# Decode attention: the first K tile in two halves, a quarter of one half on eight DMA engines, and a shorter list of slots that go straight into the result

## The chip, the cores and the metric

The kernel runs on one core of one Trainium2 chip. The metric is the time of one execution on the device in microseconds (us). The profiles are of one execution each, and their span, from the first instruction to the last, is a little shorter than that time.

## The reference: one query position against 65,536 keys

There are 32 query heads and 8 groups of keys and values; four query heads share a group. For each head the kernel forms scores against 65,536 keys of 128 numbers, takes a softmax over them, and sums the values with these weights. All inputs are bf16.

```python
B, Hq, Hkv, Sq, Sk, D = 1, 32, 8, 1, 65536, 128
...
def reference(q, k, v):
    ...
    k = jnp.repeat(k, rep, axis=1)
    v = jnp.repeat(v, rep, axis=1)
    scale = D ** -0.5
    scores = jnp.einsum("bhqd,bhkd->bhqk", q, k) * scale
    p = _softmax(scores, axis=-1)
    return jnp.einsum("bhqk,bhkd->bhqd", p, v)
```

K and V are 134 MB each and are read once. There is one query position, so there are few operations for each byte that is read.

## The kernel before

K and V of a group come in four tiles each (`j`), 64 tiles in all. A tile has 128 partitions; each holds `T` = 128 consecutive keys of `D` = 128 numbers, one contiguous row of 32 KB, so a tile is 4 MB. All tiles share a pool of five buffers, and SyncE issues the loads in the order of use:

```python
    iopool = ctx.enter_context(tc.tile_pool(name="iopool", bufs=5))
    ...
    def load(view, name, cuts=()):
        t = iopool.tile([P, T * D], bf16, name=name, tag="io")
        edges = [0, *cuts, T]
        for lo, hi in zip(edges, edges[1:]):
            nc.sync.dma_start(out=t[:, lo * D:hi * D], in_=view[:, lo * D:hi * D])
        return t

    q4 = const.tile([P, D], bf16)
    for a in range(NQ):
        nc.scalar.dma_start(out=q4[a * QP:(a + 1) * QP, :], in_=q[0, :, 0, :])

    seq = [("k", 0, j) for j in range(NQ)]
    for g in range(Hkv):
        for s in range(NQ):
            if g + 1 < Hkv:
                seq.append(("k", g + 1, s))
            seq.append(("v", g, s))
```

The query is loaded four times by ScalarE's queue, 32 rows each, transposed, and written into `Z`, from which TensorE takes its weights. A K tile is transposed by VectorE in four parts, and each part is multiplied by TensorE:

```python
    def k_step(g, j):
        kt = load(k_view[g, j], "kt")
        ...
        for i2 in range(0, NI, 2):
            kT = ktp.tile([P, 2 * CW * D], bf16, name="kT")
            nc.vector.transpose(
                out=kT[:, :].bitcast(i32),
                in_=kt[:, i2 * CW * D:(i2 + 2) * CW * D].bitcast(i32),
            )
            # [cut: eight matmuls with weights Z into S]
```

After four K tiles of a group come its softmax (`E`) and, beside the K tiles of the next group, the products of E with its V tiles into the PSUM tiles `A`. `collect` sums the parts of `A` into `ps_f`, four rows of 128 numbers, and `store` scales these and writes them out. The last V tile of all is handled apart. It comes in five pieces, of 64, 32, 16, 8 and 8 of the 128 slots (a slot is one of the `T` keys in each partition):

```python
    CUTS = (T // 2, 3 * T // 4, 7 * T // 8, T - T // 16)   # 64, 96, 112, 120
    EDGE = CUTS[-2]                                         # 112
    ...
    def store(g, ps_f, dma):
        o = stats.tile([HPG, D], bf16, name="o")
        nc.vector.tensor_scalar_mul(out=o[:, :], in0=ps_f[:, :], scalar1=rl_tiles.pop(g)[:, :])
        dma.dma_start(out=out[0, g * HPG:(g + 1) * HPG, 0, :], in_=o[:, :])

    def last_step(g, j):
        vt = load(v_view[g, j], "vt", CUTS)
        ...
        ps_f = collect(g, False)
        for t in range(EDGE):
            s = t % NQ
            slot(t, Dp[s * QP:s * QP + HPG, :], t < NQ, t >= EDGE - NQ)
        Ds = stats.tile([P, D], fp32, name="Ds")
        nc.vector.tensor_copy(out=Ds[:, :], in_=Dp[:, :])
        for t in range(EDGE, CUTS[-1]):
            slot(t, ps_f[:, :], False, False)
        nc.tensor.matmul(
            out=ps_f[:, :], lhsT=selh[:, :], rhs=Ds[:, :], start=False, stop=False
        )
        for t in range(CUTS[-1], T):
            slot(t, ps_f[:, :], False, t == T - 1)
        o = stats.tile([HPG, D], bf16, name="o")
        nc.scalar.mul(o[:, :], ps_f[:, :], rl_tiles.pop(g)[:, :])
        nc.scalar.dma_start(out=out[0, g * HPG:(g + 1) * HPG, 0, :], in_=o[:, :])
```

`slot` is one matmul of 128 columns. The first 112 slots are summed in the PSUM tile `Dp`, in four separate strips of partitions; VectorE copies `Dp` into `Ds`, and one product with `selh` adds its strips into `ps_f`. The last 16 slots go into `ps_f` without this detour.

Of the kernel before, what the change touches and what calls it, by code (L numbers as in the profile page):

```python
# [13 lines left out]
bf16 = mybir.dt.bfloat16  # L14
# [4 lines left out]
def kernel(  # L19
# [19 lines left out]
    nc = tc.nc  # L39
    P = nc.NUM_PARTITIONS  # L40
    B, Hq, Sq, D = q.shape
    _, Hkv, Sk, _ = k.shape
    HPG = Hq // Hkv
    assert B == 1 and Sq == 1 and D == P and HPG == 4 and Hq == 32
    NQ = 4
    QP = 32
    T = Sk // (NQ * NQ * QP)
# [7 lines left out]
    iopool = ctx.enter_context(tc.tile_pool(name="iopool", bufs=5))  # L55
# [4 lines left out]
    stats = ctx.enter_context(tc.tile_pool(name="stats", bufs=2))  # L60
# [4 lines left out]
    k_view = k[0].rearrange("g (j p t) d -> g j p (t d)", j=NQ, p=P)  # L65
    v_view = v[0].rearrange("g (j p t) d -> g j p (t d)", j=NQ, p=P)
# [5 lines that stand above are left out]
            nc.sync.dma_start(out=t[:, lo * D:hi * D], in_=view[:, lo * D:hi * D])  # L72
        return t

    q4 = const.tile([P, D], bf16)
    for a in range(NQ):
        nc.scalar.dma_start(out=q4[a * QP:(a + 1) * QP, :], in_=q[0, :, 0, :])
# [2 lines left out]
    for g in range(Hkv):  # L80
# [9 lines left out]
        out=sel[:, :], in_=ident[:, :].rearrange("p (s c) -> p c s", s=NQ),  # L90
        axis=AX.X, op=ALU.add,
    )
    selh = const.tile([P, HPG], fp32)
    nc.vector.tensor_reduce(
        out=selh[:, :], in_=sel[:, :].rearrange("p (i h) -> p h i", h=HPG),
# [11 lines left out]
    for a in range(NQ):  # L107
        r = slice(a * QP, (a + 1) * QP)
        z0 = QP - HPG + a * QP
        for b in range(2):  # L110
            for e in range(2):
                nc.vector.tensor_copy(  # L112
                    out=Z[r, b, e, :, z0:z0 + HPG], in_=qT_v[r, b, e, :, :]
# [4 lines left out]
    rl_tiles = {}  # L118
    A_tiles = {}

    def k_step(g, j):
        kt = load(k_view[g, j], "kt")
        if j == 0:
            S_tiles[g] = pss.tile([P, NQ, 512], fp32, name="S")
        S = S_tiles[g]
# [6 lines that stand above are left out]
            kT_v = kT[:, :].rearrange("q (i c b p e) -> q i b e c p", i=2, b=2, p=QP, e=2)  # L132
            for i in (i2, i2 + 1):
                w0 = QP - HPG - i * HPG
                for be in range(4):
                    b, e = be // 2, be % 2
                    nc.tensor.matmul(  # L137
                        out=S[:, j, :NCOL],
                        lhsT=Z[:, b, e, g, w0:w0 + P],
                        rhs=kT_v[:, i - i2, b, e, :, :],  # L140
                        start=(i == 0 and be == 0),
                        stop=(i == NI - 1 and be == 3),
                    )
# [38 lines left out]

    last_a = NQ - 2
    CUTS = (T // 2, 3 * T // 4, 7 * T // 8, T - T // 16)
    EDGE = CUTS[-2]

    def v_step(g, j):
        vt = load(v_view[g, j], "vt")
# [20 lines left out]
    def collect(g, stop):  # L209

        A = A_tiles.pop(g)
        As = [apool.tile([P, HI, D], fp32, name=f"As{u}") for u in range(2)]
        nc.scalar.copy(out=As[0][:, :, :].rearrange("p i d -> p (i d)"), in_=A[0][:, :])  # L213
        nc.vector.tensor_copy(out=As[1][:, :, :].rearrange("p i d -> p (i d)"), in_=A[1][:, :])  # L214
        ps_f = psm.tile([HPG, D], fp32, name="ps_f", tag="misc")
        for i in range(NI):
            nc.tensor.matmul(  # L217
                out=ps_f[:, :], lhsT=sel[:, i * HPG:(i + 1) * HPG],
                rhs=As[i // HI][:, i % HI, :],
                start=(i == 0), stop=(stop and i == NI - 1),  # L220
            )
        return ps_f
# [10 lines that stand above are left out]
        E = E_tiles.pop(g)  # L233
        Dp = psm.tile([P, D], fp32, name="Dp", tag="misc")
        nc.vector.memset(Dp[:, :], 0.0)

        def slot(t, dst, start, stop):
            i, c = t // CW, t % CW
            nc.tensor.matmul(
                out=dst, lhsT=E[:, j, c, i * HPG:(i + 1) * HPG],  # L240
                rhs=vt[:, t * D:(t + 1) * D], start=start, stop=stop,
# [5 lines that stand above are left out]
            slot(t, Dp[s * QP:s * QP + HPG, :], t < NQ, t >= EDGE - NQ)  # L247
        Ds = stats.tile([P, D], fp32, name="Ds")
        nc.vector.tensor_copy(out=Ds[:, :], in_=Dp[:, :])
        for t in range(EDGE, CUTS[-1]):  # L250
            slot(t, ps_f[:, :], False, False)
        nc.tensor.matmul(
            out=ps_f[:, :], lhsT=selh[:, :], rhs=Ds[:, :], start=False, stop=False
        )
        for t in range(CUTS[-1], T):
            slot(t, ps_f[:, :], False, t == T - 1)
        o = stats.tile([HPG, D], bf16, name="o")
        nc.scalar.mul(o[:, :], ps_f[:, :], rl_tiles.pop(g)[:, :])
        nc.scalar.dma_start(out=out[0, g * HPG:(g + 1) * HPG, 0, :], in_=o[:, :])

    for kind, g, s in seq:
        if kind == "k":
            k_step(g, s)
            if s == NQ - 1:
                softmax(g)
        else:
            if g == Hkv - 1 and s == NQ - 1:
                last_step(g, s)
            else:
                v_step(g, s)  # L270
                if s == NQ - 1:
                    store(g, collect(g, True), nc.scalar)
# [30 lines left out]
```

## Time and profile before

| | |
|---|---|
| time, median of 3 | 635.35 us (634.92 to 635.39) |
| span of the profiled execution | 633.6 us |
| read from HBM | 268.47 MB, 424 GB/s over the span |
| TensorE busy | 393.8 us (62%) |
| VectorE busy | 341.0 us (54%) |
| ScalarE busy | 22.8 us (4%) |
| mean granted TensorE clock | 0.814 |

In the profile PE stands for TensorE, DVE for VectorE, ACT for ScalarE and SP for SyncE, and a name with a q behind it is the sequencer of that engine. L and a number is a line of the kernel: L128 transposes K, L239 is the matmul of a slot, L252 the product with `Ds`, L258 the last scaling. The page divides the span into 40 equal slices and gives the busy share of each engine in tenths, and for the DMA engines also the rate. The chain that ended last is followed back from the last instruction, at each step to what released it. A wait is printed as: engine and line, what it waited for, us in total, times, longest.

### The profile page before, as it was taken

The numbers are of one execution on the slowest core, as the hardware profiler recorded it, in microseconds if no ns is written. First come the engines' busy times: TensorE is split into PE (matmuls) and PEld (weight loads), VectorE is DVE, ScalarE is ACT, GpSimd is POOL, SyncE is SP. The second block draws the span as 40 slices with busy tenths as digits, with TensorE's granted clock in tenths as the row PEclk, the third lists the DMA queues.
The fourth block names the chain that finished last, engine by engine and source line by source line (L and its number), as shares of the span: only waits on it lengthen the run. The fifth ranks groups of instructions, "written<-read, shape, count | busy, mean of one in ns | idle before, by whom it ended". The sixth has DMA issues, their size and how long they took to land.

```text
span 633.6 us, 5209 instructions
## 1 busy us (share of the span) xinstructions
PE 393.8 (62%) x2314; PEld 158.1 (25%) x2314; DVE 341.0 (54%) x213; ACT 22.8 (4%) x26; POOL 4.9 (1%) x7
## 2 busy tenths in 40 slices
PE   0586666767467665477753776547775577755745
PEld 0232222223122321123221232212321133211323
DVE  0898753766437753467533675345754366553600
ACT  0000100010000100010000100001000010000100
POOL 3000000000000000000000000000000000000000
PEclk9999798758788777986778977789677886877867
DMA  9999999999999999999999999999999999999995
GB/s 370 441 432 430 439 427 432 429 432 427 436 429 430 430 429 430 429 430 430 431 429 429 434 432 430 433 432 432 431 430 429 430 429 430 429 436 430 434 420 220
DMA packets 10071, 268.82 MB, mean 424 GB/s; under 512 B 1344, under 2 KB 1344, under 8 KB 1728
## 3 DMA queue, kind: packets, MB, share of 16 engines
q1 hardware_dynamic: 9792, 268.44, 98.7%
q8 instruction: 18, 0.29, 0.2%
q10 hardware_dynamic: 256, 0.04, 0.0%
q14 instruction: 5, 0.04, 0.0%
HBM read 268.47 MB, written 0.01 MB: 424 GB/s over the span
## 4 chain that ended last, share of the span: by engine, by line
DMA 52%; PE 23%; DVE 17%; issue 7%; ACT 1%; ACTq 0%; SPq 0%; DVEq 0%
DMA kt<-in_k_dram 43%; PE S L137 17%; DVE kT L128 13%; DMA vt<-in_v_dram 6%; PE ps_f L217 3%; PE A L201 2%; DMA q<-in_q_dram 2%; DVE mx L148 2%; DVE As L214 1%; ACT ET L168 1%; PE ps_b L163 0%; DVE o L226 0%; DVE Z L112 0%; PE ps_t L150 0%; PE ps_l L176 0%
## 5 line engine op out<-in xcount | busy, mean ns | idle before, releaser
L137 PE MATMUL S<-kT,Z 128*128 128x512 bf16 x1024 | 294.6, 445 | 187.9 <-DVE kT L128 187.6
L128 DVE STREAM_TRANSPOSE kT<-kt 128x2048 int32<-128x2048 int32 x128 | 289.3, 2292 | 197.6 <-DMA kt<-in_k_dram 155.1
L137 PEld LDWEIGHTS <-Z 128*128 128x128 bf16 x1024 | 111.0, 109 | 370.2 <-issue 295.3
L201 PE MATMUL A<-vt,E 128*32 128x512 bf16 x992 | 67.4, 402 | 10.9 <-DMA vt<-in_v_dram 10.9
L201 PEld LDWEIGHTS <-E 128*32 128x32 bf16 x992 | 26.6, 100 | 47.6 <-issue 27.7
L173 DVE STREAM_TRANSPOSE E<-ET 128x2048 bf16<-128x2048 bf16 x8 | 18.5, 2311 | 17.4 <-ACT ET L168 17.4
L148 DVE TENSOR_REDUCE mx<-S 128x1 f32<-128x2048 f32 x8 | 18.3, 2292 | 15.9 <-PE S L137 15.9
L217 PE MATMUL ps_f<-As,sel 128*4 128x128 f32 x128 | 26.3, 393 | 0.3 <-ACT As L213 0.3
L213 ACT COPY As<-A 128x512 f32<-128x512 f32 x8 | 4.7, 586 | 520.0 <-PE A L201 520.0
L168 ACT ACTIVATE ET<-S,nm 128x2048 bf16<-128x2048 f32 x8 | 15.7, 1968 | 78.4 <-DVE nm L165 78.4
L217 PEld LDWEIGHTS ps_f<-As,sel 128*4 128x4 f32 x128 | 14.6, 118 | 9.4 <-ACT As L213 1.2
L214 DVE COPY As<-A 128x512 f32<-128x512 f32 x8 | 5.5, 692 | 20.6 <-PE A L201 20.2
L176 PE MATMUL ps_l<-ls,selh 128*4 128x1 f32 x16 | 1.5, 165 | 19.1 <-ACT ET L168 19.1
L163 PE MATMUL ps_b<-one,mrow 1*128 1x1 f32 x16 | 3.2, 268 | 10.8 <-DVE mrow L157 10.8
L102 DVE STREAM_TRANSPOSE qT<-q 128x64 int32<-128x64 int32 x1 | 0.2, 245 | 15.9 <-DMA q<-in_q_dram 15.9
L226 DVE TENSOR_SCALAR o<-ps_f,rl 4x128 bf16<-4x128 f32 x7 | 2.4, 339 | 8.3 <-PE ps_f L217 8.3
L150 PE MATMUL ps_t<-ident,mx 128*1 128x128 f32 x8 | 2.2, 270 | 6.3 <-DVE mx L148 6.3
L163 PEld LDWEIGHTS ps_b<-one,mrow 1*128 1x128 f32 x16 | 2.5, 198 | 13.0 <-DVE mrow L157 13.0
L176 PEld LDWEIGHTS ps_l<-ls,selh 128*4 128x4 f32 x16 | 0.7, 84 | 19.8 <-ACT ET L168 19.8
L106 POOL MEMSET Z<- 128x4992 bf16 x1 | 4.3, 4263 | 0.0
L152 DVE TENSOR_REDUCE m<-ps_t 1x4 f32<-1x128 f32 x8 | 2.2, 273 | 2.5 <-PE ps_t L150 2.5
L165 DVE COPY nm<-ps_b 128x1 f32<-128x1 f32 x8 | 1.3, 158 | 4.0 <-PE ps_b L163 4.0
(23 smaller groups left out, 17.0 us busy)
## 6 DMA issues: line engine op xcount, KB each, us to landing
kt<-in_k_dram SPq DMA_DIRECT2D x32, 4096.0 KB, 43.0
vt<-in_v_dram SPq DMA_DIRECT2D x31, 4096.0 KB, 38.0
vt<-in_v_dram SPq DMA_DIRECT2D x1, 2048.0 KB
vt<-in_v_dram SPq DMA_DIRECT2D x1, 1024.0 KB
vt<-in_v_dram SPq DMA_DIRECT2D x1, 512.0 KB
vt<-in_v_dram SPq DMA_DIRECT2D x2, 256.0 KB
out_dram<-o ACTq DMA_DIRECT2D x8, 1.0 KB
q<-in_q_dram ACTq DMA_DIRECT2D x4, 8.0 KB, 6.0
```

The source lines that it names most:

```text
L106: nc.gpsimd.memset(Z[:, :, :, :, :], 0.0)
L128: nc.vector.transpose(out=kT[:, :].bitcast(i32), in_=kt[:, i2 * CW * D:(i2 + 2) * CW * D].bitcast(i32),)
L137: nc.tensor.matmul(out=S[:, j, :NCOL], lhsT=Z[:, b, e, g, w0:w0 + P], rhs=kT_v[:, i - i2, b, e, :, :], start=(i == 0 and be == 0), stop=(i ...
L148: nc.vector.reduce_max(out=mx[:, :], in_=S[:, :, :NCOL], axis=AX.XY)
L163: nc.tensor.matmul(out=ps_b[:, :], lhsT=mrow[:, :], rhs=one[:, :], start=True, stop=True)
L168: nc.scalar.activation(out=ET[:, :].rearrange("p (a n) -> p a n", a=NQ), in_=S[:, :, :NCOL], func=ACT.Exp, bias=nm[:, :], scale=SCALE, acc ...
L173: nc.vector.transpose(out=E[:, :, :, :].rearrange("p a c r -> p (a c r)"), in_=ET[:, :])
L201: nc.tensor.matmul(out=A[u][s * QP:(s + 1) * QP, :], lhsT=E[:, j, c, :], rhs=vt_v[:, u, c, :, :], start=(j == 0 and c0 == 0), stop=(j == e ...
L213: nc.scalar.copy(out=As[0][:, :, :].rearrange("p i d -> p (i d)"), in_=A[0][:, :])
L214: nc.vector.tensor_copy(out=As[1][:, :, :].rearrange("p i d -> p (i d)"), in_=A[1][:, :])
L217: nc.tensor.matmul(out=ps_f[:, :], lhsT=sel[:, i * HPG:(i + 1) * HPG], rhs=As[i // HI][:, i % HI, :], start=(i == 0), stop=(stop and i == ...
L226: nc.vector.tensor_scalar_mul(out=o[:, :], in0=ps_f[:, :], scalar1=rl_tiles.pop(g)[:, :])
```

## The change

The first K tile is no longer one load of 128 rows by 32 KB. Its first half (slots 0 to 63) is one load of 128 rows by 16 KB. Of its second half, rows 0 to 95 are one load, and rows 96 to 127 are four loads of eight rows each, every fourth row: 96, 100, ..., 124, then 97, 101, ..., and so on. The loads of eight rows are meant for DMA engines 0 to 7 alone, so that these carry more bytes of this tile than engines 8 to 15, and the 16 engines finish the whole stream closer together.

At the other end, `EDGE` moves from 112 to 120: the fourth piece of the last V tile goes into `Dp` with those before it, and only the last eight slots go straight into `ps_f`. The product with `Ds` is now the last of the sum, and the result is scaled by VectorE and stored by SyncE, through the same `store` as for the other groups (those by ScalarE's queue), where ScalarE did both for the last group. All else stands in the same order on each engine.

```diff
+    def load_first(view, name):
+        t = iopool.tile([P, T * D], bf16, name=name, tag="io")
+        h, p0 = T * D // 2, P - QP
+        nc.sync.dma_start(out=t[:, :h], in_=view[:, :h])
+        nc.sync.dma_start(out=t[:p0, h:], in_=view[:p0, h:])
+        for r in range(4):
+            nc.sync.dma_start(out=t[p0 + r::4, h:], in_=view[p0 + r::4, h:])
+        return t
 ...
     def k_step(g, j):
-        kt = load(k_view[g, j], "kt")
+        kt = (load_first if g == j == 0 else load)(k_view[g, j], "kt")
 ...
-    EDGE = CUTS[-2]
+    EDGE = CUTS[-1]
 ...
         nc.vector.tensor_copy(out=Ds[:, :], in_=Dp[:, :])
-        for t in range(EDGE, CUTS[-1]):
+        for t in range(EDGE, T):
             slot(t, ps_f[:, :], False, False)
         nc.tensor.matmul(
-            out=ps_f[:, :], lhsT=selh[:, :], rhs=Ds[:, :], start=False, stop=False
+            out=ps_f[:, :], lhsT=selh[:, :], rhs=Ds[:, :], start=False, stop=True
         )
-        for t in range(CUTS[-1], T):
-            slot(t, ps_f[:, :], False, t == T - 1)
-        o = stats.tile([HPG, D], bf16, name="o")
-        nc.scalar.mul(o[:, :], ps_f[:, :], rl_tiles.pop(g)[:, :])
-        nc.scalar.dma_start(out=out[0, g * HPG:(g + 1) * HPG, 0, :], in_=o[:, :])
+        store(g, ps_f, nc.sync)
```

The loads that SyncE issues wait for the transfer that used the same semaphore eight transfers earlier: in the changed kernel the third load of eight rows waits for the first transfer of q, the fourth for the second, the second K tile for the third, and the third K tile for the fourth.

## The prediction

> **What bounds the kernel now.** I read the page first: the forty slices, the DMA queues and the chain that ended last.
>
> ```profile
> DVE  0898753766437753467533675345754366553600
> DMA  9999999999999999999999999999999999999995
> GB/s 370 441 432 430 439 427 432 429 432 427 436 429 430 430 429 430 429 430 430 431 429 429 434 432 430 433 432 432 431 430 429 430 429 430 429 436 430 434 420 220
> ...
> q1 hardware_dynamic: 9792, 268.44, 98.7%
> q8 instruction: 18, 0.29, 0.2%
> q10 hardware_dynamic: 256, 0.04, 0.0%
> q14 instruction: 5, 0.04, 0.0%
> ```
>
> The DMA engines are busy in every slice but the last, at 427 to 441 GB/s; VectorE and TensorE are not. So what counts is when the last of 16 engines delivers its last byte, and what follows. Then the chain in order of time, at both ends, says what those are:
>
> ```profile
> 2.12 14.56 DMA q<-in_q_dram
> ...
> 19.55 2.23 DVE kT L128
> ```
>
> ```profile
> 591.74 37.29 DMA vt<-in_v_dram
> 629.03 0.04 issue
> 629.07 0.61 PE ps_f L239 x8
> 629.68 0.22 PE ps_f L252 x2
> 629.90 0.46 PE ps_f L239 x8
> 630.36 0.02 issue
> 630.38 0.36 ACT o L258
> ```
>
> The columns are start, duration and holder. At the head, compute waits 14.56 us for q and starts on K at 19.55. At the tail, the fourth piece of the last V tile lands at 629.03 and 1.7 us of work follows; the store then takes the rest of the 633.6 us span. The third reading is the waits of the queue that issues the loads:
>
> ```profile
> SPq L72 <- DVE kT L128: 365.9, 32, 19.5
> SPq L72 <- PE A L201: 98.0, 27, 4.5
> ```
>
> It waits for buffers (total, times, longest), but loads take about 40 us from issue to landing (the page's list of issues: 43.0 for K, 38.0 for V), four tiles' worth, so these waits leave no hole in the GB/s row.
>
> Fourth, what the sums hide, from the trace's records of packets and of semaphore landings. A 32 KB packet takes 1.22 us (mean of 8064), so a half row of 16 KB takes 0.61 us. Every tile gives each engine the same bytes, yet the engines drift apart: the fifth K tile, at 51 us, lands within 0.5 us on 15 engines. The last piece of V lands like this (us from the span's start, in order of time):
>
> ```
> 624.96 624.98 625.00 625.05 625.11 625.22 625.62
> 627.82 627.90 627.98 627.99 628.08 628.09 628.11 628.32 629.67
> ```
>
> Seven engines are early, nine late by about 3, one of the nine by 4.7. The 16 KB instruction packets (q8) explain it: one every 24 to 44 us, 1.02 to 1.11 us long, their lengths repeating with a period of eight, and after each one another engine lags by some 1.4 us. Eight engines thus take two each; the seventeenth (612.85 us) makes the latest. Which eight? The store of group 6 is four packets, and three of them (607.22, 607.24, 607.37) sit exactly two 1.22 us packets behind completions of early engines; the fourth belongs to a late one. [...]the early ones are, by all appearance, engines 0 to 7 but one, and the late ones 8 to 15 and that one. I call it X; the 8 KB packets of q14 fit its lag.
>
> [...]No view names an engine[...]. [...]q is 12 packets per engine (8 of data, 4 completions), each behind one of 1.22 us, 12 x 1.22 = 14.6 us, against 14.56 measured. [...]32 KB in 1.22 us is 27 GB/s per engine[...].
>
> **The change part by part.**
> (1) The split. Of the second half, 96 rows over 16 engines are 6 half rows each; four loads of 8 give engines 0 to 7 four more. Engines 0 to 7 carry 8 + 6 + 4 = 18 half rows instead of 16, engines 8 to 15 carry 14: +2 x 0.61 = +1.22 us and -1.22 us, if nothing else limits them. That is meant to take back a lag of 3. The late eight would end at 626.6 to 627.1 and the latest at 629.67 - 1.22 = 628.45. The six early ones go to at most 626.84. But X gets the addition too: 627.9 + 1.22 = 629.12 becomes the last landing. Gain 629.67 - 629.12 = 0.55 us. Sixteen-KB packets cost about 10 ns more each (4 KB takes 0.165 us, 2 KB 0.082); eight are 0.1 us, within the error.
> (2) The head. q's 12 packets now follow packets of 0.61 us: about 7.3 us instead of 14.6, so the first transpose starts near 12.5 us instead of 19.55. Off the path: worth nothing while the transfers are unbroken.
> (3) The tail. Before, the final 0.61 + 0.22 + 0.46 us of TensorE start at the fourth piece (629.03) and cover the landing of the fifth (629.67). Now the fourth piece's 8 slots go to Dp, the copy of Dp (0.29) can run beside the last 8 slots, and the product with Ds comes last. After the last landing: 0.04 + 8 slots 0.6 + product 0.25 + 0.02 + VectorE's scaling 0.34 (its row for the other groups) = 1.25 us. From 629.12 this gives 630.37, against 630.74 before: -0.37. The store from SyncE is issued in 0.33 us where ScalarE took 0.26: +0.07. Sum -0.3.
>
> **The rivals.**
> A, engines set the rate: the sum above, 635.35 - 0.3 = 635.05 us. For it: equal bytes and unequal ends, with the lag following the instruction packets.
> B, [...]the split adds collisions. [...]engines 0 to 7 fall back by about 4.9 us (3.7 to 6.1 by engine), while engines 8 to 15 lose 2.44 and gain 1.22. Early ones would end near 630.5, X at 627.9 + 3.7 to 4.9, that is 631.6 to 632.8, and the latest of the others near 629.67 + 1.22 = 630.9. With 632.3 and the same tail of 1.25 plus 0.07: 633.6 against 630.74, so +2.9, 638.2 us.[...]
> C, a hole in the stream: the third 8-row load waits for q's first transfer, the fourth for the second, the second K tile for the third. With rounds of 0.61 us the third lands near 8.3 us; engines 8 to 15 have work until 1.75 + 0.69 + 14 x 0.61 = 11.0 (0.69 is how much longer the first packet took). An issue lands its first packet about 1.0 us later (0.74 to 1.75 in this trace). Margin 1.7 us, so I expect no hole; it would add about 1 us.
> D, the earlier head counts: at most 19.55 - 12.5 = 7 us, 628 us. The full DMA row and the 40 us of loads in flight speak against it.
>
> **Range and chances.** I give B 55 in 100, A 40, the rest to C and D. That is two heaps, at 635.05 and 638.2; the mean, 636.8, is my prediction, a little slower. The range goes from just under A to above B, 634.6 to 639.2. Two per cent are 12.7 us: even B with a hole and D stay within. Chances: faster 0.01, within 0.98, slower 0.01.
>
> **What would show it right or wrong.** The first transpose near 12.5 us and an unchanged end would confirm (2). The last piece's landings decide between A and B: under A the seven move later by 1.2 and the late ones earlier by 1.2; under B both move later, the seven by 4 to 5. Under B, 16 KB packets around 7 to 17 us take up to 1.2 us instead of 0.61, under A none. A gap between packets near 11 us is C. The tail must hold, after the last landing, 8 slots, 2 products and VectorE's scaling in about 1.25 us. I am wrong if packets stretch elsewhere, if X lies in the other half[...], or if the time leaves the range.

## The result and the profile after

The changed kernel takes 640.79 us (median of 6, 640.67 to 641.32) beside 635.29 us for the kernel before in the same runs: a ratio of 1.0089, 95% interval 1.0076 to 1.0102. That is 5.5 us slower. The prediction had the direction and, in its rival B (the split adds collisions, 55 chances in 100), the kind of cause, but neither its 636.8 us nor B's 638.2 us nor the range up to 639.2 us held.

The page of the changed kernel, the forty slices and the DMA queues:

```profile
DVE  1698655565455653566543766337653467544510
DMA  9999999999999999999999999999999999999995
GB/s 264 394 426 425 427 444 437 426 427 425 428 443 432 433 427 426 427 437 433 434 431 426 428 434 431 432 431 435 428 433 432 431 425 439 430 433 431 426 422 228
...
q1 hardware_dynamic: 9976, 268.44, 98.7%
q8 instruction: 18, 0.29, 0.2%
q10 hardware_dynamic: 248, 0.04, 0.0%
q14 instruction: 4, 0.03, 0.0%
```

The bytes are the same, and from the third slice on the rate is what it was (431 GB/s in the mean of the third to the last but one, in both). The loss is in the first two slices: 264 and 394 GB/s instead of 370 and 441. A slice is 16 us long, so they moved (370 - 264 + 441 - 394) x 16 = 2,450 KB less, which is 5.7 us at 430 GB/s. The DMA row does not show it: it reads 9 there as well. The DMA engines count as busy as before and deliver less.

The busy time by stretch narrows it down. The columns are the stretch, its length, the busy time of PE, its weight loads, DVE, ACT and POOL with counts, the granted clock, the DMA share and the rate. First the kernel before, then the changed one:

```profile
8.00:13.00 5.00, 0.00 (x0) 0.00 (x0) 0.00 (x0) 0.00 (x0) 0.00 (x0) 1.00 0.99 422
14.00:18.50 4.50, 0.00 (x0) 0.00 (x0) 1.56 (x14) 0.00 (x0) 0.00 (x0) 1.00 1.00 431
21.00:31.00 10.00, 8.51 (x27) 3.10 (x27) 8.08 (x5) 0.00 (x0) 0.00 (x0) 1.00 0.99 426
```

```profile
8.00:13.00 5.00, 0.00 (x0) 0.00 (x0) 0.00 (x0) 0.00 (x0) 0.00 (x0) 1.00 1.12 257
14.00:18.50 4.50, 0.00 (x0) 0.11 (x1) 1.77 (x14) 0.00 (x0) 0.00 (x0) 1.00 0.84 171
21.00:31.00 10.00, 7.91 (x24) 2.90 (x24) 8.25 (x5) 0.00 (x0) 0.00 (x0) 1.00 0.98 419
```

From 8 to 13 us the 96-row load runs, from 14 to 18.5 us the four loads of 8 rows beside the next tile. (Bytes are booked in the stretch where a packet begins, so short stretches are rough.) The two stretches move 257 and 171 GB/s where they moved 422 and 431, at a DMA share of 1.12 and 0.84, and from 21 us on the rate is nearly that of before. The records of the packets say the same: after the first one on each engine, 16 KB packets took 0.61 us in the first half of the tile, and 112 of the 128 in its second half took 0.9 to 1.4 us; 16 packets of 32 KB that engines 8 to 15 moved for the next tile took 2.4 to 2.6 us instead of 1.22.

The chain of the changed kernel in order of time, head and tail:

```profile
2.13 10.86 DMA q<-in_q_dram
12.98 0.02 issue
13.00 36.05 DMA kt<-in_k_dram
```

```profile
605.89 29.37 DMA vt<-in_v_dram
635.26 0.04 issue
635.30 1.01 PE ps_f L250 x8
636.31 0.44 PE ps_f L263 x2
636.75 0.03 issue
636.78 0.34 DVE o L237
```

The last landing moved from 629.67 to 635.26 us: 5.6 of the 5.7 us by which the span grew (633.6 to 639.3). What comes after it is nearly as long as before, 639.3 - 635.26 = 4.0 us against 633.6 - 629.67 = 3.9.

The waits of the loads' queue have not changed in kind (total us, times, longest), so nothing holds the stream back from that side:

```profile
SPq L72 <- DVE kT L139: 359.4, 32, 20.0
...
SPq L72 <- PE A L212: 98.0, 27, 4.5
```

**Who lost how much.** The semaphore landings of the second K tile, from the trace's records: before, all 16 engines between 22.24 and 22.74 us. In the changed kernel, two groups of eight:

```
27.00 27.00 27.05 27.06 27.14 27.24 27.25 27.36      (mean +4.7 us)
29.38 29.39 29.41 29.43 29.45 29.48 29.51 29.62      (mean +7.0 us)
```

They are 2.3 us apart, close to 4 x 0.61 = 2.44 us: the four half rows that engines 0 to 7 carry more than engines 8 to 15. So the eight later ones are those that carried the loads of 8 rows: in this trace each of these loads has a group of eight landings (15.89 to 16.36 us for the first), where the 96-row load has 16 (14.56 to 15.58). No record gives an engine's number; engines 0 to 7 is the name of those eight here, 8 to 15 of the others. The bytes did move between the engines as meant, on top of a loss common to all 16 of about (4.7 + 7.0) / 2 = 5.8 us. At the end the two delays persist. The last piece of V lands at

```
629.55 629.76 631.96 631.98 632.03 632.12 632.59 632.61
632.65 632.67 632.75 632.77 634.41 634.93 635.05 635.26
```

Set against the list in the prediction, with +4.7 for one group and +7.0 for the other, this fits only if two of the seven early engines belong to 8 to 15 and five to 0 to 7, and if of the nine late ones three belong to 0 to 7 (634.93, 635.05, 635.26) and six to 8 to 15. The packets of this trace say the same by another way: on one engine a packet's record starts 3 or 4 ns before the end of the one ahead of it, so each engine can be followed from the second tile to the last piece. The 16 KB instruction packets fall on six of the eight early-landing engines of the second tile (8 to 15) and on two of the eight later ones (0 to 7); one more of 0 to 7 has three of the 8 KB ones instead and is late as well. That one is X.

### The profile page after: what moved, and what is told of

Its sections match the earlier page's. It is cut to its first block, busy times and chain, and to the rows that moved or that the text cites. A ratio compares the mean times of both kernels' runs of the same rounds, so it can differ in the third digit from the quotient of the medians.

```text
span 639.3 us, 5216 instructions
## 1 busy us (share of the span) xinstructions
PE 394.3 (62%) x2314; PEld 158.2 (25%) x2314; DVE 341.6 (53%) x214; ACT 22.4 (4%) x25; POOL 4.9 (1%) x7
## 4 chain that ended last, share of the span: by engine, by line
DMA 64%; PE 18%; DVE 12%; issue 5%; ACT 0%; ACTq 0%; DVEq 0%
DMA kt<-in_k_dram 50%; PE S L148 13%; DMA vt<-in_v_dram 11%; DVE kT L139 9%; PE A L212 2%; PE ps_f L228 2%; DVE mx L159 2%; DMA q<-in_q_dram 2%; ACT ET L179 0%; DVE As L225 0%; PE ps_b L174 0%; DVE o L237 0%; PE ps_t L161 0%; ACTq L88 0%; PE ps_f L250 0%
## 5 line engine op out<-in xcount | busy, mean ns | idle before, releaser
L184 DVE STREAM_TRANSPOSE E<-ET 128x2048 bf16<-128x2048 bf16 x8 | 18.5, 2311 | 17.4 <-ACT ET L179 17.4
L225 DVE COPY As<-A 128x512 f32<-128x512 f32 x8 | 5.5, 691 | 18.9 <-PE A L212 18.5
L250 PE MATMUL Dp<-vt,E 128*4 128x128 bf16 x120 | 2.7, 218 | 1.6 <-DMA vt<-in_v_dram 1.6
(22 smaller groups left out, 15.6 us busy)
```

The costliest lines, as they stand in the source:

```text
L184: nc.vector.transpose(out=E[:, :, :, :].rearrange("p a c r -> p (a c r)"), in_=ET[:, :])
```

## The experiments

Four theories were to be told apart. P, after the prediction's rival B: loads hold each other up, depending on the partitions that they go to and on their number of rows, and then run at about half speed. T: part of the loss is the new tail. S or R: the loss is in small pieces or in the number of loads, wherever they go. B (in this section only, and not the prediction's B): the unequal bytes of the engines are the loss. All runs are compared with the kernel before on the same chip; ratios are of times, with 95% intervals.

### The two halves of the change, each alone

**Loads alone**: the changed first K tile with the tail of before.

```diff
-        kt = load(k_view[g, j], "kt")
+        kt = (load_first if g == j == 0 else load)(k_view[g, j], "kt")
```

> The changed loading of the first K tile with the tail of the kernel before. Theory P[...]: the whole loss is here, 635.3 + 5.5 = 640.8 us, and 16 KB packets from 8 to 18 us take about 1.15 us. Rival T (a part of the loss is the new tail, whose last slots ran at half the clock): at least 0.6 us less, 640.1.

Measured: 641.1 us, ratio 1.0089 (1.0074 to 1.0104), the same as the whole change. **Tail alone**: `EDGE = CUTS[-1]`, the product with `Ds` last, and `store` from SyncE.

> The loads of the kernel before with the changed tail. Theory P: 635.3 to 635.5 us, as the slower last slots and the quicker store about cancel. Rival T: 635.9 us or more.

Measured: 635.26 us, ratio 0.9998 (0.9990 to 1.0007). The whole loss is in the loads; T falls. The slow last slots of the changed kernel, 1.01 us for eight where this run needed 0.61, come with a granted clock of half. The stretches of the changed kernel from 634 us:

```profile
634.00:635.30 1.30, 0.68 (x24) 0.39 (x24) 0.29 (x1) 0.00 (x0) 0.00 (x0) 0.99 0.13 44
635.30:636.80 1.50, 1.44 (x10) 0.93 (x9) 0.02 (x1) 0.00 (x0) 0.00 (x0) 0.50 0.00 0
```

The clock reads 0.50 in the second. With the tail alone it stayed at 1.00 at that place:

```profile
629.81 0.04 issue
629.86 0.61 PE ps_f L239 x8
630.46 0.23 PE ps_f L252 x2
630.69 0.02 issue
630.72 0.34 DVE o L226
```

So the new tail can run at the full clock. Whether it runs at half the clock more often is open: of the three profiles with the new tail, two had the product with `Ds` at half the clock (0.44 us here and in the last run below, 0.23 above), and none of the twelve with the old tail had (0.22). In the changed kernel the store landed sooner (1.2 us after its issue, 2.0 before, where an 8 KB instruction packet ran for 0.58 us from 631.41), which about paid it back.

### Halves without a split of rows

```diff
-        kt = load(k_view[g, j], "kt")
+        kt = load(k_view[g, j], "kt", (T // 2,) if g == j == 0 else ())
```

> First K tile in two halves of 128 rows each, nothing moved between engines, tail of before. Theory P: [...]no stretched packets, 635.3 us, although the first transpose starts some 7 us earlier. Rival S (the loss comes from 16 KB pieces or from more loads at the start): 1 us or more above before.

Measured: 635.5 us, ratio 1.0002 (0.9993 to 1.0011). Its stretches:

```profile
8.00:13.00 5.00, 0.00 (x0) 0.11 (x1) 2.10 (x18) 0.00 (x0) 0.00 (x0) 1.00 1.11 474
14.00:18.50 4.50, 3.27 (x8) 1.11 (x8) 3.83 (x4) 0.00 (x0) 0.00 (x0) 1.00 0.89 386
```

There are 16 KB packets here too, those of the second half took 0.61 us each, and the rate over both stretches is whole (474 and 386 beside 422 and 431), so S falls for the pieces. VectorE and TensorE are at work from 13 to 18.5 us (first transpose at 12.87 us, 19.55 before), and 6.7 us of earlier start are worth nothing. That is rival D of the prediction, answered.

### The 96 rows without moved bytes

```diff
         nc.sync.dma_start(out=t[:, :h], in_=view[:, :h])
         nc.sync.dma_start(out=t[:p0, h:], in_=view[:p0, h:])
-        for r in range(4):
-            nc.sync.dma_start(out=t[p0 + r::4, h:], in_=view[p0 + r::4, h:])
+        nc.sync.dma_start(out=t[p0:, h:], in_=view[p0:, h:])
```

> Second half of the first K tile as 96 rows and one load of 32 rows, so that each of 16 engines still gets 6 + 2 half rows: no bytes move between engines. Theory P: the 96 rows lose 2.8 us on all engines as in the changed kernel, the 32 rows[...] another 2 x 0.61 = 1.2: 635.3 + 4.0 = 639.3 us. Rival B (the loss comes from the unequal bytes of engines 0 to 7 and 8 to 15): 635.3 us.

Measured: 640.18 us, ratio 1.0074 (1.0059 to 1.0089). With equal bytes on all engines most of the loss stands; B falls as its cause. The stretch of the 96 rows is as slow as in the changed kernel (257 GB/s there):

```profile
8.00:13.00 5.00, 0.00 (x0) 0.00 (x0) 0.00 (x0) 0.00 (x0) 0.00 (x0) 1.00 1.10 247
```

The time is 0.9 us more than P's sum: the 96 rows lost more than the 2.8 us that I had read off the packets.

### The same load, into other partitions and on its own

Extra loads, issued just ahead of the first V tile (j = 0) of group 3, counted from 0, go into a buffer of the pool that nothing reads; they run at about 283 us. They are work that the kernel does not need; only their cost is looked at.

```diff
+    def extra():
+        t = iopool.tile([P, T * D], bf16, name="xt", tag="io")
+        view = k_view[0, 0]
+        for r in range(4):
+            nc.sync.dma_start(out=t[96 + r::4, :], in_=view[96 + r::4, :])
 ...
     def v_step(g, j):
+        if (g, j) == (3, 0):
+            extra()
         vt = load(v_view[g, j], "vt")
```

> Extra work in mid-stream that nothing reads: four loads of 8 whole rows (32 KB each) of K into partitions 96 to 127, every fourth. Engines 0 to 7 get 4 x 1.22 = 4.88 us more. Theory P: [...]engines 0 to 7 lose 9.8 us and engines 8 to 15 4.9; the latest of engines 0 to 7 ends at 628.1 + 9.8 = 637.9 instead of 629.67: 635.3 + 8.2 = 643.5 us. Rival R (such loads cost what they cost wherever they land): 628.1 + 4.88 = 633.0, 638.6 us, and the same as with partitions 0 to 31.

Measured: 645.03 us, ratio 1.0148 (1.0133 to 1.0163). With `t[r:32:4, :]` and the same rows of `view` instead:

> The same four extra loads of 8 rows, into partitions 0 to 31, every fourth[...]. Theory P: no stretched packets, engines 0 to 7 lose 4.88 us, engines 8 to 15 nothing: 635.3 + 3.3 = 638.6 us. Rival R: the same time as with partitions 96 to 127.

Measured: 638.24 us, ratio 1.0041 (1.0026 to 1.0055). The same number of loads, rows and bytes costs 9.4 us in one place of SBUF and 2.6 in the other. Partitions 96 to 127, then 0 to 31, in the stretch of the extra loads:

```profile
285.00:297.00 12.00, 7.95 (x29) 3.57 (x30) 7.81 (x6) 1.35 (x2) 0.00 (x0) 0.50 0.96 205
```

```profile
285.00:297.00 12.00, 7.84 (x28) 3.44 (x29) 7.70 (x6) 1.46 (x2) 0.00 (x0) 0.50 1.00 429
```

205 GB/s against 429, at a DMA share of 0.96 and 1.00. (The clock of 0.50 is TensorE's; it is the same in both.) R falls.

Then one load of 64 rows, first into partitions 0 to 63:

```diff
+        nc.sync.dma_start(out=t[:64, :], in_=view[:64, :])
```

> Extra load in mid-stream of 64 whole rows into partitions 0 to 63 (4 rows on each of 16 engines[...]). Theory P: half speed, 4 x 2.44 = 9.8 us on all engines, 645.1 us. Rival R: 4 x 1.22 = 4.9 us, 640.2 us.

Measured: 647.17 us, ratio 1.0181 (1.0165 to 1.0196). And with `t[32:96, :]` and the same rows of `view`:

> The same extra load of 64 rows, into partitions 32 to 95[...]. Theory P with rows dealt out in blocks[...] 4.9 us on all, 640.2 us. Theory P with rows dealt out in another way: packets stretched, up to 645.1 us. Rival R: 640.2 us.

Measured: 640.27 us, ratio 1.0073 (1.0058 to 1.0088). Partitions 0 to 63, then 32 to 95:

```profile
285.00:297.00 12.00, 7.83 (x28) 3.50 (x29) 7.70 (x6) 1.47 (x2) 0.00 (x0) 0.50 1.00 216
```

```profile
285.00:297.00 12.00, 7.67 (x28) 3.50 (x29) 7.53 (x6) 1.63 (x2) 0.00 (x0) 0.50 1.01 434
```

216 GB/s is half of 434. Between about 280 and 305 us, 99 packets of 32 KB took over 1.35 us in the first and one in the second (an instruction packet's neighbour). The source rows move with the partitions in these pairs, but rows 0 to 31 and rows 32 to 95 were each read at the full rate and rows 0 to 63 at half, so the source is not the cause. And as the second load cost 4.65 us, no more than the 4.9 us of its bytes, taking a buffer of the pool cost nothing.

### The 96 rows in two places, and 48

The one thing that P as I had it could not say is why all 16 engines went at about half speed under the 96-row load. Two estimates of mine, G1 with some engines at full pace and G2 with all of them losing alike, were put to the test with 96 extra rows, in two places:

```diff
+        nc.sync.dma_start(out=t[32:, :], in_=view[32:, :])     # first run
+        nc.sync.dma_start(out=t[:96, :], in_=view[:96, :])     # second run
```

> Extra load in mid-stream of 96 whole rows into partitions 32 to 127, 6 rows on each engine, 7.3 us without collisions. Theory G2[...]: four rows of each engine collide with none[...]: 9.8 us on all engines, 645.1 us, and about 32 packets of 2.4 us. Theory G1[...]: engines 0 to 5 keep 7.3 us, the others lose 9.8 to 13.4, the latest ends near 642: 647 to 649 us, and packets of 2.4 us on engines 6 to 15 only, from the first row on. Rival R[...]: 642.6 us.

Measured: 652.65 us, ratio 1.0267 (1.0253 to 1.0281).

> The same extra load of 96 rows into partitions 0 to 95. Theory G2: [...]6 x 2.44 = 14.6 us on all 16 engines, 650 us or, as the 64-row load lost a fifth more than its sum, 652; no engine keeps its pace. Theory G1: engines 11 to 15 keep 7.3 us, the rest lose 9.8 to 14.6. Rival R: 642.6 us.

Measured: 651.06 us, ratio 1.0244 (1.0230 to 1.0258). G2 (650 to 652 us) had the second run right, but missed the first by 7.5 us. G1 missed the first by 3.7 us and more, and in the second it had engines 11 to 15 keep their pace: from 284 to 301 us no packet of any engine kept its 1.22 us, in either run. All 16 engines are slow wherever the 96 rows lie. A third estimate, G3, has 96 rows at half speed on all engines in both places, 64 rows as they were found, and 48 rows at a quarter:

```diff
+        nc.sync.dma_start(out=t[:48, :], in_=view[:48, :])
```

> Extra load in mid-stream of 48 whole rows into partitions 0 to 47, 3 rows on each engine, 3.7 us without collisions. Theory G3[...]: [...]a quarter of the speed, 3 x 4.88 = 14.6 us on all engines, 650 us, with packets near 4.9 us. Theory G1[...]: [...]3 x 2.44 = 7.3 us, 643 us, packets up to some 2.5 us. Rival R[...]: 639.2 us.

Measured: 650.84 us, ratio 1.0241 (1.0224 to 1.0258), for half of the bytes of the 96-row load. The stretch of the extra load, with 96 rows (0 to 95) and with 48:

```profile
285.00:297.00 12.00, 8.23 (x32) 3.81 (x33) 8.78 (x6) 1.07 (x2) 0.00 (x0) 0.72 1.00 224
```

```profile
285.00:297.00 12.00, 7.60 (x28) 3.43 (x29) 7.46 (x6) 1.70 (x2) 0.00 (x0) 0.50 1.09 131
```

224 GB/s is about half of the 434 that stood under 64 rows at 32 to 95, 131 not much more than a quarter of it (109). With 48 rows, 44 packets took 4.0 to 4.9 us, with rows 0 to 95 none over 2.6. G3's 650 us was stated before this run and it holds; G1 and R do not. The quarter also speaks against a coarser limit, one rate for each half of the partitions: rows 0 to 47 would then run at half, as rows 0 to 63 did. No other row count was tried, and no record names the rows that an engine takes: G3 fits the three that were, and why they differ was not shown. One thing G3 leaves open: its sum for 96 extra rows is 650 us wherever they lie, and rows 32 to 127 took 652.65 us, with 18 packets of 2.6 to 3.8 us.

### The change mirrored, and the candidate

The 96 rows are now 32 to 127, and the loads of 8 are rows 0 to 31, where the extra loads of 8 rows left the full rate (429 GB/s); the same bytes are moved.

```diff
-        h, p0 = T * D // 2, P - QP
+        h, p0 = T * D // 2, QP
...
-        nc.sync.dma_start(out=t[:p0, h:], in_=view[:p0, h:])
-        for r in range(4):
-            nc.sync.dma_start(out=t[p0 + r::4, h:], in_=view[p0 + r::4, h:])
+        nc.sync.dma_start(out=t[p0:, h:], in_=view[p0:, h:])
+        for r in range(4):
+            nc.sync.dma_start(out=t[r:p0:4, h:], in_=view[r:p0:4, h:])
```

> The change mirrored: the 96 rows are 32 to 127, and the four loads of 8 rows are rows 0 to 31[...]; the same bytes move from engines 8 to 15 to engines 0 to 7. Tail of before. Theory P with G2: the 96 rows lose 1.2 us, the loads of 8 nothing, the late ones of engines 0 to 7 end at 628.1 + 1.2 + 1.2 = 630.5 instead of 629.7: 636.1 us, 4.5 us less than the change. Rival B (the moved bytes themselves are the loss): as slow as the change, 640.8 us.

Measured: 638.8 us, ratio 1.0052 (1.0037 to 1.0068). With the same bytes moved, and as many loads of the same sizes, it loses 3.3 us instead of 5.5: B falls again as the whole cause, though the moved bytes are 1.22 us of the sum below, and the number of loads falls with it. P's 636.1 us was written down with G2 and missed by 2.7 us. With G3, worked out after the run, the 96 rows lose 6 x 0.61 = 3.66 us, the loads of 8 none, and the late ones of engines 0 to 7 end at 628.1 + 3.66 + 1.22 = 632.98; its last landing is at 632.99. The second tile landed 2.4 us later than before on eight engines and 4.7 us on the other eight, against 3.66 - 1.22 = 2.44 and 3.66 + 1.22 = 4.88. Its stretches show one slow part where the change has two:

```profile
8.00:13.00 5.00, 0.00 (x0) 0.00 (x0) 0.00 (x0) 0.00 (x0) 0.00 (x0) 1.00 1.10 244
14.00:18.50 4.50, 0.00 (x0) 0.10 (x1) 2.61 (x15) 0.00 (x0) 0.00 (x0) 1.00 1.14 455
```

What can be kept of the change is the halves and the tail, each free of the loss:

> The candidate without the row split: first K tile in two halves of 128 rows, and the changed tail. Theory P: no loss, 635.2 us, the same as before within 0.1%.

Measured: 635.24 us, ratio 0.9995 (0.9987 to 1.0003). No difference from before is shown. No version here beats the kernel before.

## Why the prediction was wrong, point by point

- **The bound** was right: the last landing sets the end, and 5.6 of 5.7 us lie there. (Two small readings were off: the busy slices run from 370 and 420 GB/s, the first and the last but one, and 16 KB packets cost about 5 ns more each, 0.613 us against half of 1.215 at the median, not 10.)
- **Step (1), the split, and rival B.** Rival A's step, that the engines alone set the rate, failed: packets took about double their time under the new loads. In B the loss by the loads of 8 rows was sized right: four half rows at double time on both sides, 4 x 0.61 = 2.44 us for all. The term of B that failed is the 96 rows. Of its 4.9 us for engines 0 to 7, 1.22 are the bytes moved to them and 2.44 the loads of 8 rows; the other 1.22 were its estimate for the 96 rows, with nothing for engines 8 to 15. In the trace all 16 engines lose (112 of the 128 half rows took 0.9 to 1.4 us): 6 x 0.61 = 3.66 us at double time for every packet. That is a little too much, as each engine's first packet of this load took only 0.6 to 0.9 us. The sum is then 3.66 + 2.44 + 1.22 = 7.3 us for engines 0 to 7 (measured 7.0 at the second tile) and 3.66 + 2.44 - 1.22 = 4.9 for engines 8 to 15 (measured 4.7). With 96 and 32 rows it is 3.66 + 1.22 = 4.9 (measured 4.7). Late engines of 0 to 7: 628.1 + 7.3 = 635.4, against a last landing of 635.26. B had 631.6 to 632.8.
- **Who was late.** "The early ones are, by all appearance, engines 0 to 7 but one" was wrong. It came from three early packets and one late one of a store, and no record gives the numbers of the engines that a store uses. In the trace after, three of engines 0 to 7 were late, X and two with instruction packets, and six of engines 8 to 15. So even under rival A a move of 1.22 us to engines 0 to 7 would have pushed three of the late finishers back, where the prediction allowed for X alone.
- **The weights.** B alone stood at 638.2 us; 45 chances in 100 for the others drew the prediction to 636.8. Even all the weight on B would have left it 2.6 us short, about the term mis-sized above (3.66 - 1.22 = 2.44). The trace before could not decide between A and B, as every large load in it goes to all 128 partitions, and its 32 KB packets take 1.22 us.
- **Step (2), the head.** The first transpose came at 20.15 us, not 12.5: in the changed kernel it waited for the loads of 8 rows, the last of which landed near 20.1. With halves alone it came at 12.87 us, as worked out, and was worth nothing, as predicted.
- **Step (3), the tail.** The -0.3 us contain the 0.55 us that step (1) was to gain. The tail by itself is 1.25 + 0.07 us in the prediction's sum, against 630.74 - 629.67 = 1.07 before: +0.25. Alone it took 1.25 us from the last landing (629.81) to the end of the scaling (631.06), as worked out; its time had a ratio of 0.9998 (0.9990 to 1.0007), which holds +0.25 us as well as nothing.
- **Rival C**: there was no hole. The second K tile was issued at 9.1 us, long before engines 8 to 15 came to the end of the 96 rows near 14 us, and its first packets start at 13.9 us.

## What to carry to other kernels

DMA engines that show as busy may deliver half (205 GB/s at a share of 0.96 here, 429 at 1.00): compare the rate, not the share, and look at how long packets of one size take. No version here gained by moving bytes from one engine to another. A load of fewer than 128 rows went at the full rate here in some places only: loads of 8 rows left 429 GB/s at partitions 0 to 31 and 205 at 96 to 127, one of 64 rows 434 at 32 to 95 and 216 at 0 to 63. Before bytes are moved to even out finishing times, each late engine has to be named, not guessed from a few.

## What the runs showed of the hardware

- What partitions a load goes to can halve the rate of all DMA engines: a 64-row load at partitions 0 to 63 left 216 GB/s, at 32 to 95 434 GB/s.
- The number of rows matters too: from partition 0 on, 64 rows left 216 GB/s, 96 rows 224 and 48 rows 131, so that 48 extra rows cost as much as 96 (+15.4 and +15.6 us).
- Collisions in mid-stream cost more than their sum: 11.6 us where 9.8 was worked out for 64 rows, 9.4 where 8.2 was for the loads of 8 rows, with 99 and 100 packets stretched instead of 64. At the start of the stream, where the landings of a load lay within 0.5 us before, the sums fit (7.3 and 4.9 us for 7.0 and 4.7).
- The 16 engines drift apart by up to 4.7 us over 630 us, by some 1.4 us after each 16 KB instruction packet, and the lags were still there at the last landings.
